# A table of 470 moved jobs in the recorded order of a gated recurrence fused with a multiplicative feed-forward layer

## The chip, the cores and the metric

The kernel runs on one core of a Trainium2 chip. The metric is device time in microseconds. Before the change the median of five runs is 530.94 us (530.24 to 532.46).

## The reference

The first stage is a gated linear recurrence over 4 sequences of 5824 steps with 256 channels; the second is a feed-forward layer without an activation, on the 23296 resulting rows.

```
a_t = exp(8 * sigmoid(r_gate) * log(sigmoid(a_param)))        # decay, per step and channel
x_gated = sqrt(max(1 - a_t*a_t, 1e-6)) * sigmoid(i_gate) * x
h = a_t * h + x_gated                                          # over the steps; y = all h
out = (((y @ w1) * (y @ w2)) @ w3) @ w_out                     # 256 -> 1024 -> 1024 -> 256
```

## The kernel before

The rows are cut into 46 chunks: chunk 0 has 256 rows, all others 512. Channels lie on the 128 partitions in two halves for the scan. The product of w3 and w_out is formed once on the chip (the "fold"), so that each chunk needs two up products of 256 by 1024 and one down product of 1024 by 256.

Every piece of work is a job, 2032 in all. For chunk c the jobs are:

- loads r, i, x on the SP queue (L171), each 512 KB; SP also issues the stores and the DMA transpositions (turn_dma, L228);
- on ACT: tanh_r and tanh_i (L179, L189), decay in two halves (the exponential, L235), root (L251, the square root, which needs another function table than tanh and exponential), four copies of an up product from PSUM (copy, L313, through L311) and two copies of the down product (evac);
- on POOL: plus and two halves of times (sigmoid of i times x, L195 to L214), two squares of the decay (L244), and the cast of y to bf16 (L288); for some early chunks DVE does times, squares or the cast;
- on DVE: gated (L261), two scans (L273), and four products g = pa * pb (L319, called product c,mp);
- on PE: turn_r and turn_u as matrix transpositions for some early chunks (L216; the others go by DMA), four pairs pa and pb of up products (L294), four downs (L326).

The fold has, for each of 8 pieces of w3, a load, a cast on POOL, fold_t (transposition on PE), fold_c (copy to SBUF on DVE), fold_m (product with w_out on PE) and fold_e (copy of the result to wp_sb on DVE, L416).

A planner inside the kernel gives each job a due time and a duration, and picks jobs for each engine by due time when their inputs and buffers are free in its own clock (L594 to L634). The list of jobs by planned start, `plan`, is then recorded job by job; nothing at run time changes the order. Each engine does its own jobs strictly in the recorded order, with waits on semaphores for inputs from other engines and for buffers. So a job that is put ahead of another on an engine holds it up if it must itself wait. SP's queue works in the same manner: a store that waits for its data holds all loads behind it.

The buffers that connect the engines: pa and pb share three PSUM buffers (tag pab), given out in recorded order; a buffer of pa is free after copy, one of pb after product. Two PSUM buffers (tag po) serve the downs, the transpositions on PE and the fold. There are 3 buffers for each of r, i, x, 6 for decay, root and the transposed u, 4 for y, 3 for g and 3 for output tiles.

A group of chunks shares one table switch: all roots of a group (for example chunks 12 to 16) stand together on ACT, and the first of them needs the squares of the whole group. Before up products in the first 80 us, small matmuls on the identity (L299) are put in where the planner saw PE idle; their number is fixed by the planner, before the table is used.

The place where the order can be altered by hand already exists; with an empty table it does nothing:

```
    places = {p for p, _ in MOVES}
    rest = [key for p, key in enumerate(plan) if p not in places]
    for p, to in MOVES:
        rest.insert(to, plan[p])
```

Of the kernel before, what the change touches and what calls it, by code (L numbers as in the profile page):

```python
# [20 lines left out]
def kernel(  # L21
# [80 lines left out]
    SLOT = 10.5  # L102
    M_OCC, M_LAT, M_PE = 0.04033835273, 0.02581866041, 0.0
    WARM = 80.0
    MOVES = []
    OFFSET = {"r": 6.5, "i": 4.0, "x": 7.5, "tanh_r": 1.5, "tanh_i": 5.0, "plus": -14.0, "turn_r": -0.5,
              "turn_u": 4.0, "decay": 10.5, "square": -2.5, "root": 8.5, "gated": 10.0, "cast": 6.5,
              "copy": 2.5, "product": -3.0, "store": 5.0}
# [531 lines left out]
    plan = [key for _, _, key in sorted(order)]  # L640
# [4 lines that stand above are left out]
# [37 lines left out]
```

## Time and profile before

| | |
|---|---|
| median of 5 runs | 530.94 us |
| profiled execution | 530.74 us, span 528.9 us |
| PE busy | 497.1 us (94%) |
| ACT busy | 456.7 us (86%) |
| DVE busy | 442.8 us (84%) |
| POOL busy | 342.4 us (65%) |
| HBM over the span | 78.91 MB read, 23.86 MB written |
| granted TensorE clock | 1.00 |

The time of the profiled execution is that of the whole run; its span goes from the first to the last instruction. In the page's slices each digit is the busy share of one fortieth of the span, about 13.2 us. A line of a timeline gives start, duration, engine, line, operation, what it writes from what it reads, and in brackets how long the engine was idle before it and what ended that. Names in the trace: ptr is a transposition on PE, ptw and pw are the fold's PSUM tiles, pa and pb the up products, po the down product, nrm the squares, roots and gated inputs, h_t the scan's result, y_t its bf16 cast, g_t the product.

### The profile page before, as it was taken

To read this page: it belongs to the slowest core of one execution; us is meant where nothing else is said; L and a number is where in the kernel's file an instruction comes from. 1 tells how busy PE (TensorE), PEld (TensorE's weight loads), DVE (VectorE), ACT (ScalarE), POOL (GpSimd) and SP (SyncE) were. 2 spreads that over 40 slices of the span, in tenths; PEclk is the share of its full clock that TensorE was granted. 3 is DMA by queue.
4 is the path that set the end of the run, shared out by engine and by line. 5 is a ranking of instruction groups with operands and counts; after the bars stand their busy time and mean duration, and the time that the engine had idled before them with its cause. 6 is when DMAs were issued, how large, how long until landed. Compare 5 with 4: busy or idle time off the path is not lost.

```text
span 528.9 us, 8756 instructions
## 1 busy us (share of the span) xinstructions
PE 497.1 (94%) x3148; PEld 308.2 (58%) x3204; DVE 442.8 (84%) x376; ACT 456.7 (86%) x535; POOL 342.4 (65%) x270
## 2 busy tenths in 40 slices
PE   1299899999999999999999999999999999999997
PEld 1176676566556566556566566565665665655555
DVE  0788899998999889997889799898798988698842
ACT  5988797999899989989989989998999998965453
POOL 1569795578747768964895968878588667492100
PEclk9999999999999999999999999999999999999999
DMA  8999969899998996998897999978999876623112
GB/s 291 387 374 360 307 161 304 244 277 251 310 259 195 311 298 190 257 240 208 238 236 236 233 319 262 259 221 218 244 261 273 239 176 163 160 77 86 57 40 100
DMA packets 174604, 123.28 MB, mean 233 GB/s; under 512 B 84448, under 2 KB 170208, under 8 KB 174560
## 3 DMA queue, kind: packets, MB, share of 16 engines
q1 hardware_dynamic: 174288, 122.71, 84.8%
q8 instruction: 25, 0.41, 0.3%
q14 instruction: 19, 0.16, 0.1%
q10 hardware_dynamic: 272, 0.00, 0.0%
HBM read 78.91 MB, written 23.86 MB: 194 GB/s over the span
## 4 chain that ended last, share of the span: by engine, by line
PE 79%; ACT 8%; DMA 4%; DVE 4%; issue 4%; SPq 0%; DVEq 0%; ACTq 0%
PE po L334 26%; PE pb L303 25%; PE pa L303 25%; DMA out_dram<-ot 2%; ACT sa L311 2%; DVE g_t L323 2%; ACT a_t L242 2%; ACT nrm L258 1%; DMA rt<-th_r 1%; PE pw L399 1%; DMA r_t<-in_r_gate_dram 1%; PE ptr L221 1%; DVE h_t L284 1%; ACT th_r L183 1%; ACT th_i L192 1%
## 5 line engine op out<-in xcount | busy, mean ns | idle before, releaser
L323 DVE TENSOR_TENSOR g_t<-sa,pb 128x1024 bf16<-128x1024 bf16 (+1 forms) x184 | 219.3, 1200 | 56.2 <-ACT sa L311 41.2
L303 PEld LDWEIGHTS <-w_sb 128*128 128x128 bf16 x1472 | 144.3, 98 | 142.8 <-issue 4.0
L311 ACT CAST sa<-pa 128x1024 bf16<-128x1024 f32 (+1 forms) x183 | 182.1, 1002 | 34.7 <-PE pa L303 32.8
L303 PE MATMUL pa<-y_t,w_sb 128*128 128x512 bf16 (+1 forms) x698 | 184.3, 378 | 3.4 <-DVE g_t L323 1.7
L303 PE MATMUL pb<-y_t,w_sb 128*128 128x512 bf16 (+1 forms) x718 | 185.8, 378 | 1.4 <-DVE g_t L323 0.3
L334 PE MATMUL po<-wp_sb,g_t 128*128 128x256 bf16 x1456 | 181.0, 273 | 0.2
L334 PEld LDWEIGHTS <-g_t 128*128 128x128 bf16 x1456 | 142.4, 98 | 45.0
L284 DVE TENSOR_TENSOR_SCAN h_t<-a_t,h_t,nrm 128x512 f32<-128x512 f32 (+3 forms) x90 | 137.1, 1535 | 0.8
L213 POOL TENSOR_TENSOR u_t<-th_i,x_t 128x512 bf16<-128x512 f32 x78 | 117.8, 1528 | 0.9 <-DMA ut<-u_t 0.5
L249 POOL TENSOR_TENSOR nrm<-a_t 128x512 f32<-128x512 f32 (+1 forms) x84 | 100.1, 1206 | 14.1 <-ACT a_t L242 12.8
L292 POOL CAST y_t<-h_t 128x1024 bf16<-128x1024 f32 x40 | 50.1, 1252 | 89.0 <-DVE h_t L284 86.2
L197 POOL TENSOR_SCALAR th_i<-th_i 128x1024 f32<-128x1024 f32 x42 | 52.3, 1248 | 35.0 <-ACT th_i L192 34.9
L311 ACT COPY ot<-po 128x512 f32<-128x512 f32 (+1 forms) x89 | 51.7, 583 | 17.1 <-PE po L334 16.9
L242 ACT ACTIVATE a_t<-rt,la 128x512 f32<-128x512 bf16 x74 | 59.0, 819 | 6.7 <-DMA rt<-th_r 6.6
L269 DVE SCALAR_TENSOR_TENSOR nrm<-nrm,ut 128x1024 f32<-128x1024 f32 x39 | 55.4, 1420 | 1.7 <-DMA ut<-u_t 1.7
L192 ACT ACTIVATE th_i<-i_t 128x1024 f32<-128x1024 f32 (+1 forms) x46 | 48.4, 1052 | 1.2 <-POOL u_t L213 1.1
L258 ACT ACTIVATE nrm<-nrm 128x1024 f32<-128x1024 f32 (+1 forms) x46 | 47.4, 1055 | 0.2
L185 ACT ACTIVATE th_r<-r_t 128x1024 bf16<-128x1024 f32 x37 | 39.2, 1063 | 0.4 <-DMA r_t<-in_r_gate_dram 0.4
L221 PE MATMUL ptr<-ident,th_r 128*128 128x128 bf16 x68 | 6.9, 259 | 15.0 <-ACT th_r L183 15.0
L258 ACT ACT_TABLE_LOAD x14 | 18.0, 1283 | 0.2
L242 ACT ACTIVATE a_t<-ptr,la 128x512 f32<-128x512 bf16 (+1 forms) x18 | 12.7, 753 | 3.6 <-PE ptr L221 3.1
L221 PEld LDWEIGHTS <-th_r 128*128 128x128 bf16 x68 | 5.4, 118 | 16.4 <-ACT th_r L183 15.8
(39 smaller groups left out, 143.5 us busy)
## 6 DMA issues: line engine op xcount, KB each, us to landing
r_t<-in_r_gate_dram SPq DMA_DIRECT2D x45, 512.0 KB, 6.1
i_t<-in_i_gate_dram SPq DMA_DIRECT2D x45, 512.0 KB, 5.5
x_t<-in_x_dram SPq DMA_DIRECT2D x45, 512.0 KB, 4.9
out_dram<-ot SPq DMA_DIRECT2D x89, 256.0 KB, 3.5
wf<-in_moe_w_dram SPq DMA_DIRECT2D x12, 512.0 KB, 6.2
wf<-in_moe_w_out_dram SPq DMA_DIRECT2D x2, 512.0 KB, 7.1
ut<-u_t SPq DMA_TRANSPOSE x39, 4.9
rt<-th_r SPq DMA_TRANSPOSE x37, 5.1
```

What stands on the lines that cost most here:

```text
L192: nc.scalar.activation(out=t[:, :n, :], in_=T["i", c][:, :n, :], func=AF.Tanh, scale=0.5)
L197: nc.gpsimd.tensor_scalar(t, t, 1.0, 1.0, op0=ALU.add, op1=ALU.mult)
L213: nc.gpsimd.tensor_mul(out=u.rearrange("p cb j q -> p j cb q")[:, js], in0=cut(t)[:, js], in1=cut(T["x", c])[:, js])
L242: nc.scalar.activation(out=a, in_=pr, func=AF.Exp, scale=la4[:, cb:cb + 1], bias=la4[:, cb:cb + 1])
L249: eng.tensor_mul(out=T["n", c][:, cb, :w], in0=T["a", c][:, cb, :w], in1=T["a", c][:, cb, :w])
L258: nc.scalar.activation(out=T["n", c][:, :, :w], in_=T["n", c][:, :, :w], func=AF.Sqrt, scale=-1.0, bias=1.0)
L269: nc.vector.scalar_tensor_tensor(out=T["n", c][:, :, :w], in0=T["n", c][:, :, :w], scalar=1e-3, in1=T["pu", c][:, :, :w], op0=ALU.max, op1 ...
L284: nc.vector.tensor_tensor_scan(T["h", c][:, cb, lo:hi], T["a", c][:, cb, lo:hi], T["n", c][:, cb, lo:hi], init, ALU.mult, ALU.add)
L303: nc.tensor.matmul(out=pp[:, q, :w], lhsT=w_sb[:, cb, m * P:(m + 1) * P], rhs=T["y", c][:, cb, :w], start=(cb == 0), stop=(cb == NCB - 1))
L311: nc.scalar.copy(out=dst, in_=src_ps)
L323: nc.vector.tensor_mul(out=T["g", c][:, 2 * mp:2 * mp + 2, :w], in0=T["sa", c, mp][:, :, :w], in1=T["pb", c, mp][:, :, :w])
L334: nc.tensor.matmul(out=po, lhsT=T["g", c][:, k, j * P:(j + 1) * P], rhs=wp_sb[:, k, :], start=(k == 0), stop=(k == KD - 1), skip_group_che ...
```

## The change

The table gets 470 entries (place in the plan, place in the new list). Each named job is taken out of the plan and put in again at the given place; all others keep their relative order. The places go up to about 703 of 2032, which is the work on the early chunks. Engine, operation and data of every job stay the same. The table's start and end:

```diff
-    MOVES = []
+    MOVES = [(2, 0), (13, 4), (16, 5), (10, 6), (18, 7), (1, 9), (7, 10), (8, 15), (23, 19), (32, 20),
+             (19, 25), (22, 26), (28, 27), (25, 28), (37, 29), (21, 31), (27, 32), (39, 33), (36, 34),
+             (24, 35), (35, 39), (33, 40), (44, 41), (45, 42), (48, 49), (56, 50), (43, 52), (61, 54),
...
+             (692, 690), (682, 694), (671, 695), (690, 696), (685, 697), (676, 700), (686, 702),
+             (669, 703)]
```

What it does to single jobs, read from the order of the two programs' instructions (a place is counted within the job's own engine; the time is that of the job in the profile before):

| engine | job | place before | place after | time before, us |
|---|---|---|---|---|
| SP | load x of chunk 0 | 1 | 9 | 0.74 |
| SP | load r of chunk 2 | 8 | 4 | 4.82 |
| SP | load x of chunk 5 | 23 | 40 | 22.75 |
| DVE | squares of chunk 2 | 5, 6 | 4, 5 | 18.74 |
| DVE | times of chunk 2 | 4 | 6 | 17.50 |
| DVE | cast of chunk 0 | 13 | 10 | 26.47 |
| DVE | square 3,0 | 15 | 19 | 28.18 |
| DVE | fold_e 5 | 47 | 45 | 59.91 |
| DVE | product 8,1 | 97 | 100 | 127.33 |
| DVE | product 10,1 | 114 | 113 | 152.09 |
| PE | pa 3,3 | 64 | 54 | 73.37 |
| PE | pa 10,0 | 144 | 139 | 142.44 |
| ACT | tanh_i of chunk 4 | 19 | 29 | 26.15 |
| ACT | root of chunk 3 | 29 | 34 | 37.04 |
| POOL | squares of chunk 12 | 61, 62 | 69, 78 | 115.72, 116.82 |

## The prediction

> **What bounds the kernel now.** I read the busy shares and slices of the page first.
>
> ```profile
> PE 497.1 (94%) x3148; PEld 308.2 (58%) x3204; DVE 442.8 (84%) x376; ACT 456.7 (86%) x535; POOL 342.4 (65%) x270
> ...
> PE   1299899999999999999999999999999999999997
> ...
> DVE  0788899998999889997889799898798988698842
> ...
> PEclk9999999999999999999999999999999999999999
> DMA  8999969899998996998897999978999876623112
> ```
>
> PE is the bound and idles almost only in the first two slices and the last. So I asked for the stretches that the moved jobs cover (they end near 185 us) and the rest.
>
> ```profile
> core 0: us, PE busy (x) PEld busy (x) DVE busy (x) ACT busy (x) POOL busy (x), PEclk, DMA share, GB/s
> 0.00:27.00 27.00, 5.99 (x47) 4.71 (x48) 11.69 (x18) 21.06 (x25) 9.84 (x15) 1.00 0.93 340
> 27.00:62.00 35.00, 32.24 (x262) 22.34 (x264) 30.45 (x38) 28.50 (x34) 26.19 (x25) 1.00 1.08 344
> 62.00:127.00 65.00, 64.18 (x434) 40.98 (x440) 58.66 (x50) 59.88 (x71) 48.23 (x36) 1.00 0.91 249
> 127.00:163.00 36.00, 34.69 (x215) 21.19 (x218) 35.61 (x29) 33.12 (x40) 21.21 (x17) 1.00 1.07 284
> 163.00:185.00 22.00, 21.89 (x132) 12.82 (x132) 20.50 (x17) 20.55 (x26) 18.00 (x15) 1.00 1.01 257
> ```
>
> PE's idle time is 21.0 us before 27, 2.8 from 27 to 62, 0.8 to 127, 1.3 to 163, 0.1 to 185: 26.0 us is all that moving early jobs can reach. From 127 to 163 DVE rests only 0.4 us, so there DVE sets the pace with PE. The lines of PE's and DVE's timelines with an idle time behind them name the rest.
>
> ```profile
> 26.30 1.03 PE L221 MATMUL ptr<-ident,th_r 128*128 128x128 bf16 x8 [3.41 <-ACT th_r L183]
> 27.12 1.27 PE L299 MATMUL pa<-ident 128*128 128x128 bf16 x10
> 28.19 1.06 PE L303 MATMUL pa<-y_t,w_sb 128*128 128x256 bf16 x4
> ...
> 60.37 0.61 PE L385 MATMUL ptw<-ident,w_t 128*128 128x128 bf16 x8 [1.43 <-DVE wp_sb L416]
> ...
> 153.35 0.81 PE L303 MATMUL pa<-y_t,w_sb 128*128 128x512 bf16 x3 [1.10 <-DVE g_t L323]
> ```
>
> ```profile
> 22.92 1.26 DVE L266 SCALAR_TENSOR_TENSOR nrm<-nrm,ptr 128x512 f32<-128x512 f32 x2
> 24.10 2.45 DVE L284 TENSOR_TENSOR_SCAN h_t<-a_t,h_t,nrm 128x512 f32<-128x512 f32 x2
> 26.47 0.40 DVE L292 CAST y_t<-h_t 128x512 bf16<-128x512 f32 x1
> 26.78 1.28 DVE L266 SCALAR_TENSOR_TENSOR nrm<-nrm,ptr 128x512 f32<-128x512 f32 x2
> 28.18 1.14 DVE L249 TENSOR_TENSOR nrm<-a_t 128x512 f32<-128x512 f32 x1
> 30.21 0.69 DVE L323 TENSOR_TENSOR g_t<-sa,pb 128x512 bf16<-128x512 bf16 x1 [0.89 <-PE pb L303]
> ```
>
> The second fence is the opening: chunk 0's scans are done at 23.0, but its cast (26.47), which the first up product needs, stands behind chunk 1's gating and scans. PE starts real work at 28.19.
>
> **The change part by part.** No instruction is added or removed, and ACT still loads 31 tables. The lowered programs differ in order alone: 153 of PE's 582 jobs, 102 of DVE's 362, 135 of ACT's 503, 62 of POOL's 264 and 114 of SP's 321 stand at another place. So the cost is in waits, and I follow the new order with the old durations.
>
> *Opening loads (SP).* x of chunk 0 goes from first to ninth, r of chunk 2 and the first two weight loads go ahead. r of chunk 0 no longer follows 0.25 MB. From the landings (ACT's first tanh 5.68 after 0.5 MB issued, second 7.01 after 1.0 MB) that is 1.33 us per 0.5 MB, so r lands 0.66 us earlier; ACT, which runs without a pause from 10.85 to 17.5, moves up by about 0.6. x of chunk 0 lands after 3.75 MB instead of first: 5.68 + 3.25 x 2.66 = 14.3; its product, which ran at 10.65, is then at 14.3. It is not late: gating needs it at 21. DVE does two squares ahead of chunk 2's product, which costs most of the 0.6 back, so gating of chunk 0 stays at about 20.95 (was 21.07). I take 0.1.
>
> *The cast of chunk 0 (DVE, three places up).* Gating 0.75, two scans 1.27, cast 0.40: it ends near 23.3 instead of 26.87, and up product 0 can start near 23.9 instead of 28.19, 4.3 earlier. This isn't yet the gain. The three PSUM buffers fill, and the second pb waits for the first gating product on DVE. DVE is late by the cast: gating and scans of chunk 1 from 23.3 to 26.85, gating of chunk 2 to 28.1, product at 28.1 instead of 30.21. Of these 2.1 us, 0.68 comes from one square put behind it. On equal work DVE is 1.4 ahead, plus up to 1.2 of its own waits for PE (0.89, 0.16 and 0.16) that go: 2.6. Following PE through pa and pb of chunk 0, its last pb starts near 32.1 (was 34.75). I take 2.1, between 1.4 and 2.6: by the DVE row, since DVE's chain releases PE's buffers.
>
> *Weight fold, 44 to 66 us.* fold_e 5 now stands ahead of products 2,2 and 2,3 (2 x 1.13 us). In the old order PE waited for it, 1.43 + 0.34 by the timeline. With the move the buffer is free 2.3 us earlier, so the wait goes, unless the weight loads are late: w3 loads are issued on SP when the previous cast frees a buffer, and one is now behind the transposed r of chunk 6, which waits for its tanh (near 44 us, old load 46.7), so not later. Between 0 and 1.8 I take 1.4, near the row.
>
> *62 to 127.* Chunk 3's products go ahead of chunk 4's scans, downs are spread, stores and loads change places on SP. PE has only 0.8 idle; the part at 103 (0.29 and 0.27) falls partly: +0.2. Late loads would cost here: x of chunk 5 goes 17 SP places back, behind a DMA transposition of chunk 4, to about 53 us with its use at 66; x of chunk 9 and r of chunks 12 to 14 keep 10 us or more. Cost nothing, while those 10 us last; if they go, POOL's product is late and the transposition after it on SP, then gating and scan.
>
> *127 to 163.* Product 10,1 now comes before the cast of chunk 11 (1.6 us), which clears the 1.10 wait at 153.35, if DVE isn't late: +0.5. Against this, product 8,1 goes behind chunk 10's two scans and a square (with them 4.1 us of DVE work), while PE wants the buffer for pa 8,3 0.7 us earlier. Old times: 127.33 - 0.97 (idle) + 4.1 + 1.2 = 131.7 for its end, against 132.04 - 0.7 = 131.3 for PE. At equal leads PE waits 0.4; laid on the old slots, 1.85. I take -1.1, the middle, as PE will lead DVE a little. On POOL the two squares of chunk 12 go 8 and 16 places back, to about 146, with the group's five roots at 149 waiting for them: no cost, 3 us of cover; past these ACT waits and the two PSUM copies behind the roots with it.
>
> *The lock.* By the tile view the scans of this stretch took
>
> ```profile
> L284 DVE TENSOR_TENSOR_SCAN h_t<-a_t,h_t,nrm x29: 1140/1283/2380, 25.3 to 187.8; 128x512 f32<-128x512 f32 x27, 128x448 f32<-128x448 f32 x2
> ```
>
> so at times 1.1 us over the median. The Trainium skill, "SBUF — State Buffer", section "SBUF: two separate sides", says that DVE operations with two SBUF inputs and GpSimd operations take a shared port pair as an exclusive lock, and the loser waits for a whole instruction. So who meets whom is drawn anew by a new order, and the old durations, which I used, need not hold. By the row the sum is unchanged; by the rule, two more stretched scans in DVE's full stretch at 127 to 163 cost 2 x 1.1 = 2.2. I take the row, since stretches can also go, and keep 2.2 both ways in the range.
>
> *Sum.* 0.1 + 2.1 + 1.4 + 0.2 + 0.5 - 1.1 = 3.2 us. After 185 us the order is the same and PE idles only 2.5 us in 315, so a lead of all engines is carried to the end. The profiled execution took 530.74 (span 528.9 and 1.8 around it), 0.2 under the median of the runs: 530.74 - 3.2 = 527.5, or 527.7 beside the median.
>
> **Rivals.** (B) The head start is lost: DVE, 30.45 of 35 us busy from 27 to 62, keeps the old pace, and PE fills the time with the same waits elsewhere. For it: 35.6 of 36 us at 127. Against it: DVE idles 10 us in all between 27 and 127, which an earlier PE removes. It gives 530.3. (C) All of it comes and nothing is given back: 2.6 + 1.8 + 0.6 + 1.1 = 6.1, 524.8. Against it: product 8,1. (D) Slower: DVE comes to 122 us without a lead of its own (late products, stretched scans), and then the order there turns against PE: waits at pa 8,3 (1.85), pb 8,3 (0.64), pa 10,0 (0.54: its cast has 3.1 us more ahead, and it is itself 4.0 us earlier on PE), pb 10,0 (0.89), pb 10,1 (0.66), as the new order on old slots has them: 4.6 us, doubled where DVE is stretched by 2.2 again, with the opening's gain down to 1.4 and the fold's to 1.4: +1.8 to +4, about 533.5. It decides where DVE's lead at product 8,0 is under 2 us.
>
> **How the numbers follow.** Forecast 0.47, its own range 526.0 to 529.2; B 0.18; C 0.10; D 0.25. The predicted time is 527.7. The range from 524.9 to 534.0 leaves half of C (0.05) and the upper third of D (0.1) outside. A measurement here tells about 0.3%, 1.6 us: faster is the forecast and C and a little of B, 0.59; same is most of B and the edge of D, 0.17; slower 0.24.
>
> **What would show it.** First up matmul with y near 24, chunk 0's first gating product near 28.1, no wait of a fold transposition for wp_sb near 60, PE's idle time from 0 to 62 down from 23.8 to about 20. A wait of pa for g_t near 130 is the give-back; many of them, with DVE full, D. Wrong would be: waits of PE for y_t casts, of ACT for rt transpositions (one of 2.77 us is in the old trace) or of SP that push loads to their use.

## The result, and the profile after

| | before | changed |
|---|---|---|
| median | 531.54 us (46 runs, 528.82 to 534.34) | 528.85 us (25 runs, 525.4 to 531.26) |
| profiled execution | 530.74 us, span 528.9 us | 527.21 us, span 525.4 us |
| PE, ACT, DVE, POOL busy, us | 497.1, 456.7, 442.8, 342.4 | 495.6, 455.7, 436.4, 342.9 |

The ratio is 0.9952, with an interval of 0.9938 to 0.9966: the changed kernel is faster by 2.6 us (1.8 to 3.3). Its profiled execution lies 1.6 us under its own median, the one before 0.8 under its own, so the two profiles differ by 3.5 us and the medians by 2.7. The readings below account for the 3.5; why typical executions keep only about 2.7 of it comes in the section on the experiments.

The longer table moves all line numbers by 65: an up product is L368, the copy of pa L376, the product g L388, a scan L349, the cast of y L357, gated L331 and L334, a square L314, tanh_r L250, decay L307, a load L239.

First the page of the changed kernel: busy times, then the slices of PE, the granted clock and the DMA share.

```profile
PE 495.6 (94%) x3147; PEld 307.2 (58%) x3204; DVE 436.4 (83%) x376; ACT 455.7 (87%) x535; POOL 342.9 (65%) x270
...
PE   1489999999999999999999999999999999999997
...
PEclk9999999999999999999999999999999999999999
DMA  8989989999999997988995999959999875633113
```

PE's first slices read 1, 4, 8 and no longer 1, 2, 9: real work begins earlier, with a hole behind it. DVE is 6.4 us less busy with the same instructions. Next the stretches of the prediction, in the changed kernel.

```profile
core 0: us, PE busy (x) PEld busy (x) DVE busy (x) ACT busy (x) POOL busy (x), PEclk, DMA share, GB/s
0.00:27.00 27.00, 8.60 (x71) 7.28 (x72) 12.33 (x17) 21.42 (x26) 9.42 (x15) 1.00 0.94 349
27.00:62.00 35.00, 31.48 (x266) 20.96 (x269) 33.66 (x40) 30.31 (x36) 29.67 (x25) 1.00 0.95 302
62.00:127.00 65.00, 64.58 (x430) 41.23 (x436) 57.64 (x54) 61.46 (x74) 43.38 (x35) 1.00 1.00 270
127.00:163.00 36.00, 34.57 (x214) 21.04 (x217) 32.20 (x29) 32.24 (x37) 24.06 (x19) 1.00 1.07 289
163.00:185.00 22.00, 21.84 (x132) 13.12 (x134) 20.19 (x18) 20.41 (x26) 17.41 (x14) 1.00 1.11 280
```

From 127 to 163 DVE now rests 3.8 us instead of 0.4. That stretch was the one with both engines full, and it no longer is.

Busy time hides how much work was done in it, so I use a second measure. A PE job should take its own pace: 0.864 us for an up product of 512 columns (four matmuls), 0.875 for a down or a product of the fold, 0.445 for a transposition of eight matmuls, half for chunk 0. The small matmuls on the identity count with 0.056 us each. The start of a job to the start of the next, less that pace, is PE time lost, whether PE idled, was held up or ran slower than its pace. Summed by stretch, in us (a loss across a boundary can be split otherwise, which moves single entries by up to 0.3):

| | 0-27 | 27-45 | 45-62 | 62-127 | 127-163 | 163-185 | 185-end | sum |
|---|---|---|---|---|---|---|---|---|
| before | 24.3 | 3.5 | 2.4 | 0.6 | 1.2 | 0.0 | 1.1 | 33.1 |
| changed | 22.4 | 4.2 | 0.5 | -0.2 | 1.8 | -0.1 | 1.1 | 29.6 |
| difference | -2.0 | +0.7 | -1.9 | -0.8 | +0.5 | -0.1 | 0.0 | -3.5 |

The sum is the whole difference of the two spans, within rounding. The places show in PE's timeline of the changed kernel, in its lines with an idle time behind them.

```profile
24.41 1.01 PE L368 MATMUL pa<-y_t,w_sb 128*128 128x256 bf16 x4 [0.27 <-DVE y_t L357]
...
29.89 0.61 PE L286 MATMUL ptr<-ident,th_r 128*128 128x128 bf16 x8 [2.30 <-DVE nrm L331]
...
42.06 1.02 PE L368 MATMUL pb<-y_t,w_sb 128*128 128x512 bf16 x4 [0.39 <-DVE g_t L388]
43.57 1.04 PE L368 MATMUL pa<-y_t,w_sb 128*128 128x512 bf16 x4 [0.48 <-DVE y_t L357]
...
145.02 1.02 PE L368 MATMUL pb<-y_t,w_sb 128*128 128x512 bf16 x4 [0.26 <-DVE g_t L388]
148.90 1.02 PE L368 MATMUL pb<-y_t,w_sb 128*128 128x512 bf16 x4 [0.25 <-DVE g_t L388]
150.63 1.02 PE L368 MATMUL pa<-y_t,w_sb 128*128 128x512 bf16 x4 [0.71 <-DVE g_t L388]
```

The first up product stands at 24.41 instead of 28.19. Then PE waits 2.30 us with a transposition of chunk 4 for a PSUM buffer, which DVE's gating frees. No fold transposition waits near 60. Two small waits at 42 and 44 are new, and so are three at 145 to 151, in place of one of 1.10 at 153. DVE's timeline of the opening in the changed kernel:

```profile
21.91 1.99 DVE L349 TENSOR_TENSOR_SCAN h_t<-a_t,nrm 128x256 f32<-128x256 f32 x2
23.93 0.43 DVE L357 CAST y_t<-h_t 128x512 bf16<-128x512 f32 x1
24.28 1.28 DVE L331 SCALAR_TENSOR_TENSOR nrm<-nrm,ptr 128x512 f32<-128x512 f32 x2
25.47 3.19 DVE L349 TENSOR_TENSOR_SCAN h_t<-a_t,h_t,nrm 128x512 f32<-128x512 f32 x2
28.58 1.25 DVE L331 SCALAR_TENSOR_TENSOR nrm<-nrm,ptr 128x512 f32<-128x512 f32 x2
29.76 0.67 DVE L388 TENSOR_TENSOR g_t<-sa,pb 128x512 bf16<-128x512 bf16 x1
```

The cast stands right behind the scans of chunk 0. But those scans took 1.99 us where the old trace has 1.27, and those of chunk 1 3.19 where it has 2.45, so the first product moved only from 30.21 to 29.76. The old line of chunk 0's scans:

```profile
21.74 1.27 DVE L284 TENSOR_TENSOR_SCAN h_t<-a_t,nrm 128x256 f32<-128x256 f32 x2
```

One thing the row of the granted clock doesn't show: it reads 1.00 from the start in both pages, but its first record lies at 31.84 us before the change and at 26.13 in the changed kernel, and PE ran at half pace until then. Four matmuls on 256 columns took 1.06 us at 28.19 before and 1.01 at 24.41 in the changed kernel. After these times they take 0.60, first in the old trace and then in the new:

```profile
33.05 0.60 PE L303 MATMUL pb<-y_t,w_sb 128*128 128x256 bf16 x4
```

```profile
30.48 0.60 PE L368 MATMUL pb<-y_t,w_sb 128*128 128x256 bf16 x4
```

Of chunk 0's eight up products four ran at half pace before, and two in the changed kernel.

The lead over the kernel before, start against start, is 3.78 us at the first up product of chunk 0 (4.25 at the ten small matmuls ahead of it), 3.57 at the first up products of chunks 14, 16 and 20, 3.58 at chunk 30, 3.53 at chunk 45, and 3.52 at the last store. Behind chunk 14 nothing is gained or lost in this profile.

### The profile page after: what moved, and what is told of

Same layout as the page of the kernel before. It is cut to its first block, busy times and chain, and to the rows that moved or that the text cites. A ratio compares the mean times of both kernels' runs of the same rounds, so it can differ in the third digit from the quotient of the medians.

```text
span 525.4 us, 8727 instructions
## 1 busy us (share of the span) xinstructions
PE 495.6 (94%) x3147; PEld 307.2 (58%) x3204; DVE 436.4 (83%) x376; ACT 455.7 (87%) x535; POOL 342.9 (65%) x270
## 4 chain that ended last, share of the span: by engine, by line
PE 81%; DVE 7%; ACT 4%; issue 3%; DMA 3%; SPq 0%; ACTq 0%; DVEq 0%
PE po L399 27%; PE pa L368 26%; PE pb L368 26%; DVE h_t L349 3%; DVE g_t L388 2%; DMA rt<-th_r 2%; ACT a_t L307 1%; ACT sa L376 1%; PE pw L464 1%; DMA r_t<-in_r_gate_dram 1%; PE ptr L286 1%; ACT th_i L257 1%; PE ptw L450 1%; DVE nrm L331 1%; DVE y_t L357 0%
## 5 line engine op out<-in xcount | busy, mean ns | idle before, releaser
L388 DVE TENSOR_TENSOR g_t<-sa,pb 128x1024 bf16<-128x1024 bf16 (+1 forms) x184 | 219.6, 1200 | 62.3 <-ACT sa L376 42.1
L368 PEld LDWEIGHTS <-w_sb 128*128 128x128 bf16 x1472 | 143.6, 98 | 142.2 <-issue 4.7
L376 ACT CAST sa<-pa 128x1024 bf16<-128x1024 f32 (+1 forms) x183 | 181.8, 1003 | 39.1 <-PE pa L368 37.9
L368 PE MATMUL pa<-y_t,w_sb 128*128 128x512 bf16 (+1 forms) x703 | 183.4, 377 | 3.6 <-DVE g_t L388 1.3
L368 PE MATMUL pb<-y_t,w_sb 128*128 128x512 bf16 (+1 forms) x712 | 184.7, 377 | 2.1 <-DVE g_t L388 0.9
L349 DVE TENSOR_TENSOR_SCAN h_t<-a_t,h_t,nrm 128x512 f32<-128x512 f32 (+3 forms) x90 | 133.2, 1494 | 0.7
L278 POOL TENSOR_TENSOR u_t<-th_i,x_t 128x512 bf16<-128x512 f32 x78 | 114.0, 1479 | 3.1 <-DMA x_t<-in_x_dram 1.6
L314 POOL TENSOR_TENSOR nrm<-a_t 128x512 f32<-128x512 f32 (+1 forms) x84 | 101.2, 1220 | 11.6 <-ACT a_t L307 10.3
L357 POOL CAST y_t<-h_t 128x1024 bf16<-128x1024 f32 x40 | 50.7, 1267 | 80.0 <-DVE h_t L349 74.4
L262 POOL TENSOR_SCALAR th_i<-th_i 128x1024 f32<-128x1024 f32 x42 | 54.9, 1309 | 41.0 <-ACT th_i L257 41.0
L376 ACT COPY ot<-po 128x512 f32<-128x512 f32 (+1 forms) x89 | 51.7, 583 | 16.9 <-PE po L399 16.8
L307 ACT ACTIVATE a_t<-rt,la 128x512 f32<-128x512 bf16 x74 | 58.6, 819 | 2.1 <-DMA rt<-th_r 2.0
L334 DVE SCALAR_TENSOR_TENSOR nrm<-nrm,ut 128x1024 f32<-128x1024 f32 x39 | 53.0, 1361 | 0.7 <-DMA ut<-u_t 0.7
L250 ACT ACTIVATE th_r<-r_t 128x1024 bf16<-128x1024 f32 x37 | 39.1, 1061 | 0.4 <-DMA r_t<-in_r_gate_dram 0.3
L307 ACT ACTIVATE a_t<-ptr,la 128x512 f32<-128x512 bf16 (+1 forms) x18 | 12.8, 753 | 3.3 <-PE ptr L286 1.9
```

Source lines behind the costliest of these rows:

```text
L262: nc.gpsimd.tensor_scalar(t, t, 1.0, 1.0, op0=ALU.add, op1=ALU.mult)
L278: nc.gpsimd.tensor_mul(out=u.rearrange("p cb j q -> p j cb q")[:, js], in0=cut(t)[:, js], in1=cut(T["x", c])[:, js])
L307: nc.scalar.activation(out=a, in_=pr, func=AF.Exp, scale=la4[:, cb:cb + 1], bias=la4[:, cb:cb + 1])
L314: eng.tensor_mul(out=T["n", c][:, cb, :w], in0=T["a", c][:, cb, :w], in1=T["a", c][:, cb, :w])
L334: nc.vector.scalar_tensor_tensor(out=T["n", c][:, :, :w], in0=T["n", c][:, :, :w], scalar=1e-3, in1=T["pu", c][:, :, :w], op0=ALU.max, op1 ...
L349: nc.vector.tensor_tensor_scan(T["h", c][:, cb, lo:hi], T["a", c][:, cb, lo:hi], T["n", c][:, cb, lo:hi], init, ALU.mult, ALU.add)
```

## The experiments

The expectations weigh three readings. By the first, the one that was predicted, each stage has its own saving, from waits that can be named, and a lead once won is carried on. By the second the order works only as a whole: a part of it meets the old order at a seam and waits there. By the third (the lock of the prediction) the order matters little, and the gain is that DVE and POOL happen to meet less at their shared ports. All edits change only the table, so that the order of the jobs alone is different. The diffs show the table's size, or the order of an engine's jobs against that of the changed kernel; "lead" is again start against start with the kernel before, in the profiles.

**The first part of the new order, then the old.** Three runs keep the new order for its first 87, 230 or 460 jobs; all jobs behind these stand in the old order.

```diff
-    MOVES = [ ... ]   # 470 entries
+    MOVES = [ ... ]   # 52 entries: the first 87 jobs as in the changed list, the rest as in plan
```

> The new order for the first 87 jobs of its list alone (to the first up product of chunk 1, about 31 us), the old order for all the rest. Theory A (each stage's saving is kept by PE): the opening saves 2.2 us by chunk 1, and 1 to 2.2 of it reach the end, since the old waits at 60 and 153 us stay: 0.2 to 0.4% faster. Theory S (a stage is worth something only with the stages that follow): under 0.5 us, same. Theory L (the gain is that DVE and POOL meet less in the shared port from 62 to 185 us): 0, with DVE's stretched operations as in the kernel before.

```diff
-    MOVES = [ ... ]   # 470 entries
+    MOVES = [ ... ]   # 150 entries: the first 230 jobs as in the changed list, the rest as in plan
```

> The new order for the first 230 jobs (to about 62 us, opening and weight fold), then the old order. A: 3.2 us saved in the profile by chunk 3's first up product (opening 2.2, less 0.8 given back at chunk 2's cast, fold 1.85), 2.5 to 3.2 in the end. S: about half of the whole change, 1.3. L: at most 0.5.

```diff
-    MOVES = [ ... ]   # 470 entries
+    MOVES = [ ... ]   # 313 entries: the first 460 jobs as in the changed list, the rest as in plan
```

> The new order for the first 460 jobs (to about 117 us), then the old order. A: 4.0 us by 127 us, then the old order's wait of pa 10,3 for product 10,1 behind chunk 11's cast, which grows with PE's lead: 2.7 to 3.5 in the end. S: nearly all, 2.5. L: most of it, because 4.1 of the 6.6 us of DVE stretch that vanished lay from 62 to 127.

| | median, us | ratio to before | lead at chunk 14, us |
|---|---|---|---|
| first 87 | 532.23 | 1.0021 (1.0007 to 1.0034) | -2.8 |
| first 230 | 533.24 | 1.0048 (1.0029 to 1.0067) | -3.3 |
| first 460 | 533.15 | 1.0035 (1.0023 to 1.0048) | -2.0 |

All three are slower than the kernel before, though each has the early first up product. With the first 87 jobs, PE waits for a copy of the fold behind two squares of chunk 3, which stand together there and took 1.57 and 1.52 us instead of the usual 0.68, while POOL ran squares as well (32.56 to 35.04). PE's line and then DVE's, of this run:

```profile
36.25 1.01 PE L390 MATMUL ptw<-ident,w_t 128*128 128x128 bf16 x8 [3.01 <-DVE w3t L399]
```

```profile
32.58 3.01 DVE L254 TENSOR_TENSOR nrm<-a_t 128x512 f32<-128x512 f32 x2
35.52 0.68 DVE L399 COPY w3t<-ptw 128x1024 bf16<-128x1024 bf16 x1
```

With the first 230, a transposition that lands at 75.81 instead of 70.89 holds ACT for 4.15 us, and PE behind the copy for 2.66. ACT's line of this run, then PE's:

```profile
75.84 0.81 ACT L259 ACTIVATE a_t<-rt,la 128x512 f32<-128x512 bf16 x1 [4.15 <-DMA rt<-th_r]
```

```profile
78.08 1.66 PE L320 MATMUL pb<-y_t,w_sb 128*128 128x512 bf16 x4 [2.66 <-ACT sa L328]
```

With the first 460, ACT's tanh_i waits 5.26 us for a buffer that POOL's times has to free (124.65), and PE waits 4.34 us at 126.66 for a copy behind it. So every seam costs more than what lies ahead of it had brought. This is the second reading, and stronger than it was put: no cut that was tried gives a share of the gain.

The seams cost more than their wait, too. The windows around the first one, in the run with 87 jobs:

```profile
33.00:36.00 3.00, 0.24 (x3) 0.07 (x1) 3.00 (x3) 2.89 (x4) 3.00 (x3) 1.00 1.03 385
36.00:39.00 3.00, 2.75 (x15) 1.84 (x15) 2.49 (x4) 0.68 (x1) 0.49 (x1) 0.52 1.07 357
39.00:42.00 3.00, 3.00 (x23) 1.63 (x22) 2.97 (x4) 1.98 (x3) 1.15 (x2) 0.91 1.07 372
```

Behind the wait the granted clock is 0.52, then 0.91: 0.48 x 3 + 0.09 x 3 = 1.7 us of PE's full pace are lost on top. The same sum is 1.7 behind the seams of the other two.

**The whole order once more.** The table is the same list of jobs, written in other lines.

> The changed kernel's order again, a second profile. If its savings come from the order, PE's lead over the kernel before is again 3.6 us at 185 us within 0.7, with the same waits. If they come from chance encounters in the shared port, the stretch of DVE's operations from 27 to 185 us (8.8 us in the first profile, 15.4 before) and the lead differ by more than 1.5 us from the first profile.

528.23 us, ratio 0.9941 (0.9922 to 0.9961): the gain stands. The profiled execution (528.32) has the same waits as the one of the changed kernel up to chunk 14, where its lead is 3.51. DVE's instructions from 27 to 185 took 9.1 us more than their usual durations (scan 1.28, gated 1.21, times 1.24, cast 0.69, square 0.68 us) against 8.8 in the changed kernel and 15.4 before, so the lower figure belongs to the order and not to one execution. But 1.4 us of lead go at chunk 15, on the part of the list that is not changed. ACT's line, then PE's:

```profile
192.74 1.06 ACT L242 ACTIVATE th_r<-r_t 128x1024 bf16<-128x1024 f32 x1 [1.77 <-DMA r_t<-in_r_gate_dram]
```

```profile
194.75 1.02 PE L360 MATMUL pb<-y_t,w_sb 128*128 128x512 bf16 x4 [0.55 <-ACT sa L368]
```

tanh_r of chunk 24 waits for its load, and the next copy and PE wait behind it. In the changed kernel's profile the same instruction waited 0.32 us:

```profile
191.22 1.06 ACT L250 ACTIVATE th_r<-r_t 128x1024 bf16<-128x1024 f32 x1 [0.32 <-DMA r_t<-in_r_gate_dram]
```

**The cast of chunk 0, alone and put back.**

```diff
-    MOVES = [ ... ]   # 470 entries
+    MOVES = [(67, 57)]
```

> The old order with one job moved: the cast of chunk 0 on DVE ahead of chunk 1's gating and scans. Theory A (DVE's chain releases PE's buffers): the first up product starts near 24.3 (3.5 us earlier; a transposition on PE ahead of it that waits for ACT may hold it at 27.1), but the first gating product stays near 30.2; 0 to 0.8 us faster. Rival (PE's start counts): 2.5 us or more faster.

530.94 us, ratio 0.9997 (0.9984 to 1.001): nothing. The cast is at 23.54, yet PE cannot use it:

```profile
26.80 1.03 PE L221 MATMUL ptr<-ident,th_r 128*128 128x128 bf16 x8 [3.41 <-ACT th_r L183]
```

In the old order the transposition of chunk 3 stands on PE ahead of the first up product and waits for its tanh as before. The cast is half of a pair; the changed order also moves that transposition.

```diff
 scan 0,1
-cast 0
 gated 1
 scan 1,0
 scan 1,1
+cast 0
 gated 2
```

> The new order with the cast of chunk 0 put back behind chunk 1's second scan. A: the first up product starts near 28.5 instead of 24.4; of these 4.1 us part was spent waiting for the first gating product, which is 0.4 earlier now: 1 to 2 us slower than the changed kernel. Rival (PE's start counts): 4 us slower.

531.36 us, ratio 0.9999 (0.9984 to 1.0014): putting this one job back takes the whole gain, 2.5 us by the median of the changed kernel and 3.1 by that of its second run. PE's line in this run:

```profile
29.28 1.01 PE L360 MATMUL pa<-y_t,w_sb 128*128 128x256 bf16 x4 [4.40 <-DVE y_t L349]
```

PE was still at half pace during this wait and until 32.25 us, 6.1 later than in the changed kernel. In this profile the lead at chunk 14 is 0.78 us instead of 3.57 or 3.51, so 2.7 to 2.8 are gone by then; another 1.8 goes at chunk 15, at the load of r of chunk 24 (the table further down). The cast is necessary for the gain and not enough for it.

**The fold's step.**

```diff
 scan 3,1
-fold_e 5
 cast 3
 product 2,2
+product 2,3
+fold_e 5
 fold_c 6
-product 2,3
 fold_c 7
```

> The new order with the fifth fold result's copy (fold_e 5) put back behind products 2,2 and 2,3 on DVE. A: the transposition of fold piece 6 on PE waits again 1.4 to 1.8 us near 58 us and that reaches the end. Rival (the wait is hidden by PE's lead or by DVE being the bound): under 0.4 us.

529.36 us, ratio 0.9962 (0.9948 to 0.9976). A wait of PE is back at the same transposition, but by another path:

```profile
61.26 0.61 PE L442 MATMUL ptw<-ident,w_t 128*128 128x128 bf16 x8 [1.54 <-ACT a_t L299]
```

In this run fold_e 5 starts at 62.07, when the transposition has begun. So PE did not wait for the buffer that fold_e 5 frees. It took the other of the two, which the decay of chunk 8 on ACT freed at 61.21. What the early fold_e 5 gives is a buffer that is free sooner than that one. The lost PE time from 45 to 62 is 2.45 us against 0.5 and 0.8 in the two profiles of the changed order: 1.7 to 2.0 in its stretch. By the medians, 0.5 to 1.1 us are left of this at the end.

**Product 8,1.**

```diff
 product 7,3
+product 8,1
 scan 10,0
+product 8,2
 scan 10,1
-product 8,1
-product 8,2
 product 9,0
```

> The new order with products 8,1 and 8,2 put back ahead of chunk 10's scans on DVE. The prediction put a give-back of 1.1 us on this place: then this kernel is 1.1 faster than the changed one. By the changed kernel's trace PE doesn't wait there: 0, or a loss where chunk 10's cast comes later.

529.73 us, ratio 0.9968 (0.9954 to 0.9982): not faster than the changed kernel. The lost PE time from 127 to 163 is 2.4 us against 1.8 and 1.3 in the two profiles of the changed order, with waits at new places (0.57 at 133.53, 0.71 at 147.40). So the new place of product 8,1 is no give-back that shows; in these profiles the old place loses 0.6 to 1.1 in its stretch.

**SP's queue alone in the old order**, all other engines in the new one (482 entries).

> The new order on the four engines, the old order in SP's queue alone (114 jobs). If the load order matters (r of chunk 0 first, weights and transpositions ahead): the opening loses 0.5, and transpositions or stores that are late for the new ACT order cost 1 us or more on top, 1 to 4 slower than the changed kernel. Rival (loads are early enough either way): under 0.7 slower.

553.18 us, ratio 1.0424 (1.0396 to 1.0452): 22 us slower than before. The waits of ACT by what it waited for (us in total, times, longest), in this run:

```profile
ACT a_t L301 <- DMA rt<-th_r: 21.8, 8, 5.2
...
ACT th_r L244 <- DMA r_t<-in_r_gate_dram: 7.2, 2, 5.1
```

and in the changed kernel:

```profile
ACT a_t L307 <- DMA rt<-th_r: 2.0, 3, 1.0
```

The order of the other engines can't run without SP's 114 moved jobs. In the old SP order transpositions stand behind stores that wait for data which now comes later: SP's longest wait ahead of a store is 8.7 us here and 6.5 in the changed kernel. What SP's moves gain by themselves this run doesn't tell.

**The squares of chunk 12 on POOL.**

```diff
 cast 8
+square 12,0
+square 12,1
 times 11,0
...
 times 13,1
-square 12,0
 plus 14
...
 square 15,1
-square 12,1
 times 15,0
```

> The new order with the two squares of chunk 12 put back 8 and 16 places on POOL, ahead of the products for u. The move's cover was put at 3 us: then this is the same within 0.5. If the move is what keeps DVE and POOL apart at 114 to 130 us, DVE's stretch from 62 to 163 us rises from 5.1 us by 1 or more and the time with it.

537.88 us, ratio 1.0135 (1.0101 to 1.0168), 9.0 to 9.7 us above the changed kernel. POOL's timeline and then PE's, in this run:

```profile
118.99 1.04 POOL L306 TENSOR_TENSOR nrm<-a_t 128x512 f32<-128x512 f32 x1 [6.31 <-ACT a_t L299]
120.90 1.71 POOL L306 TENSOR_TENSOR nrm<-a_t 128x512 f32<-128x512 f32 x1 [0.87 <-ACT a_t L299]
122.57 7.68 POOL L270 TENSOR_TENSOR u_t<-th_i,x_t 128x512 bf16<-128x512 f32 x4
130.20 1.04 POOL L349 CAST y_t<-h_t 128x1024 bf16<-128x1024 f32 x1
```

```profile
131.29 1.87 PE L360 MATMUL pa<-y_t,w_sb 128*128 128x512 bf16 x4 [6.15 <-POOL y_t L349]
```

The decays of chunk 12 are 3.4 and 3.8 us later in the changed order (117.79 and 119.71 instead of 114.43 and 115.93), while POOL is there earlier. At the old place the squares wait for them, and the cast of chunk 9, which PE needs, stands behind. The late place is thus what the rest of the order needs.

**x of chunk 0 loaded first, as before.**

```diff
+load x 0
 load r 0
...
 load i 1
-load x 0
 load x 1
```

> The new order with one load put back: x of chunk 0 first in SP's queue. A: r of chunk 0 lands 0.66 us later, ACT's opening chain moves by it: 0.4 to 0.7 slower in the profile at the first up product, and 0 to 0.6 in the end.

530.49 us, ratio 0.9982 (0.9963 to 1.0002): 1.6 to 2.3 us above the changed kernel. In the profile the lead at chunk 0's first up product is 2.80 us instead of 3.78, and 3.23 in the second profile of the changed order: by single profiles 0.4 to 1.0 us of it come from the opening loads. PE left its half pace at 29.00 us in this run.

**A scan one step further up**, meant to take the three waits at 145 to 151 away.

```diff
 gated 11
+scan 11,0
 product 9,2
 product 9,3
-scan 11,0
 product 10,0
```

> A version meant to be better: the changed order with chunk 11's first scan put two places up on DVE, into the 1.22 us in which DVE waits for PE ahead of product 9,2. PE's waits at 144 to 151 us (1.7 us lost in the changed kernel's trace) fall by 1.2: 1.2 faster than the changed kernel. Rival: something else is then last (copies on ACT, the table switch ahead of the roots at 142): under 0.3.

529.06 us, ratio 0.9955 (0.9933 to 0.9977): no gain over the changed kernel. Of the three waits one of 0.21 stays, and one of 1.15 at 139.88 is new. The lead at chunk 14 is 5.29 us in this profile, the largest of all, since its opening also happened to run better (lost time from 27 to 45: 2.1 against 4.2). It didn't last: at chunk 16 the lead is 1.38. ACT's line, then PE's, then the windows, all of this run:

```profile
192.09 1.06 ACT L242 ACTIVATE th_r<-r_t 128x1024 bf16<-128x1024 f32 x1 [2.90 <-DMA r_t<-in_r_gate_dram]
```

```profile
194.09 1.02 PE L360 MATMUL pb<-y_t,w_sb 128*128 128x512 bf16 x4 [1.69 <-ACT sa L368]
195.35 1.84 PE L360 MATMUL pa<-y_t,w_sb 128*128 128x512 bf16 x4 [0.23 <-DVE g_t L380]
```

```profile
192.00:195.00 3.00, 1.31 (x6) 0.48 (x5) 0.93 (x1) 2.90 (x3) 0.00 (x0) 1.00 1.16 331
195.00:198.00 3.00, 2.77 (x10) 1.31 (x9) 3.00 (x4) 2.99 (x5) 1.37 (x1) 0.57 1.10 349
198.00:201.00 3.00, 3.00 (x22) 2.13 (x20) 1.90 (x2) 2.92 (x4) 3.00 (x4) 0.86 1.22 271
```

It is the load of r of chunk 24 again. The table compares its issue on SP with the start of the tanh:

| profile | r of chunk 24 issued | tanh_r of chunk 24 starts | ACT waited | lead at chunk 14, then 16 |
|---|---|---|---|---|
| before | 189.61 | 194.84 | 0.36 | - |
| changed | 186.22 | 191.22 | 0.32 | 3.57, 3.57 |
| again | 187.53 | 192.74 | 1.77 | 3.51, 2.12 |
| x of chunk 0 first | 188.25 | 193.51 | 1.65 | 2.61, 1.35 |
| product 8,1 put back | 189.54 | 194.60 | 1.80 | 1.68, 0.26 |
| fold_e 5 put back | 190.63 | 195.71 | 2.24 | 1.01, -0.85 |
| cast of chunk 0 put back | 190.93 | 195.92 | 2.22 | 0.78, -1.05 |
| scan 11,0 up | 186.51 | 192.09 | 2.90 | 5.29, 1.38 |

The tanh starts 5.0 to 5.6 us behind the issue in all eight, with a DMA share of 1.1 to 1.2 there. Before the change the load was already just in time, so a lead passes this point only as far as SP's queue is ahead as well. Of these seven profiles with the new order, whole or but for one change, the changed kernel's own is the only one that loses nothing here. In the changed kernel's profile SP was 3.4 ahead, in the last one 3.1 while PE was 5.3 ahead. Why SP follows less than PE in most executions is open.

**Profile and median.** This also bears on the 1.6 us between the changed kernel's profile and its median: an execution that loses 1.4 us at chunk 15, as the second profile does, is at 528.3. A second part is the clock. Each run also has its mean granted clock: 8 of the changed kernel's 25 runs had 0.996 or 0.997, with a median of 530.15, the other 17 had 0.999 or 1.0, with 528.21 (of 53 runs of the kernel before, 9 were at 0.996 or 0.997). One loss of 1.7 us in 525 is 0.003. Two profiles with the new opening, those of the fold's step and of product 8,1, show where: behind PE's wait near 29.9 (2.25 and 1.93 us in them). The windows of the fold's step put back:

```profile
27.00:30.00 3.00, 0.75 (x8) 0.54 (x7) 3.00 (x4) 2.03 (x4) 1.86 (x3) 0.94 1.01 340
30.00:33.00 3.00, 3.00 (x19) 2.35 (x18) 1.71 (x3) 0.37 (x1) 1.75 (x2) 0.50 0.89 301
```

The changed kernel's profile has 1.00 in the same windows, behind a wait of 2.30. That PE time is lost in part only (27 to 45: 5.2 and 4.7 against 4.2), since PE still waits for DVE there. How much of the 1.6 each part makes was not measured.

## Why the prediction was right

The forecast was 527.5 for the profiled execution and 527.7 for the median; they came at 527.21 and 528.85. The sign and the size hold, and the main mechanism too: the early cast, by way of DVE, and the fold's buffer. That the profile is met to 0.3 is in part luck. The opening gave less than forecast, the two next stretches gave more, the fourth lost as much as forecast by another cause, and this profile happened to keep its whole lead at chunk 15. Point by point:

- *Opening loads and the cast (0.1 + 2.1).* The opening gave 2.0 up to 27 us, and the first up product was 3.8 earlier against 4.3 forecast. But the first product is at 29.76 and not at 28.1, because four scans took 1.46 us more than in the old trace: two of them began while POOL ran, a meeting of the kind that the row on the lock put at 0. The wait that this leaves was of a transposition for a PSUM buffer of the gating, not of a second pb. Chunk 0's last pb started at 33.20 and not near 32.1. Another 0.7 was lost by 45: the changed kernel has waits of 2.30, 0.39 and 0.48 there, the last for the cast of chunk 2 (1.58 us, 2.5 us later than before). The old kernel had waits of 0.27 and 0.51 and, as an estimate, 2.4 us lost to the half pace from 27 to 31.84. The steps had no term for the later cast and none for the pace. Net, the stretch to 45 gave 1.3. PE's idle time from 0 to 62 fell from 23.8 to 21.9, not to about 20. The split was wrong as well: the loads, put at 0.1, are worth 0.4 to 1.0 of the lead, as x of chunk 0 put back alone shows; the estimate had taken most of the earlier landing away again for two squares.
- *Weight fold (1.4).* 1.9 measured, about the upper end of 1.8. A PSUM buffer that is free earlier is the mechanism forecast: with fold_e 5 put back, the same transposition waits 1.54 us at 61.26, for the other buffer.
- *62 to 127 (0.2).* 0.8 measured. DVE's instructions were stretched less there: 2.6 us over their usual durations in this stretch instead of 6.7. That this made the difference was not shown.
- *127 to 163 (+0.5 - 1.1).* The sum of -0.6 met the measured -0.5, by another cause. The step that product 8,1 makes PE wait at pa 8,3 failed: DVE was at product 8,0 at 117.08 instead of 122.14, 5.1 us ahead, and product 8,1 began at 125.85 where the working had its end at 131.7. Putting it back brings no gain. The loss is at 145 to 151: PE waits there for products of chunk 10, which stand on DVE behind the two scans of chunk 11 (2.07 and 2.85 us), and DVE's lead is down to 2.2 us at product 10,0.
- *The lock.* The row was taken, 0, with 2.2 both ways. DVE's stretch from 27 to 185 fell from 15.4 to 8.8 us, so it went, and the prediction had kept this side open. It isn't enough for a gain: the first 460 jobs have 9.2 and are slower than before, and with the cast of chunk 0 put back it is about 9 as well, at the old time. How much of the gain needs it was not shown. That the stretches come from meeting POOL is shown by the profiles, in the last section, and agrees with the exclusive lock in the section "SBUF: two separate sides" of the Trainium skill's "SBUF — State Buffer".
- *Squares of chunk 12 (no cost, 3 us of cover).* No cost, but the reason was wrong: the move isn't a free one inside a cover, it is needed, and undoing it costs 9 us.
- *"A lead of all engines is carried to the end."* This failed in general. It held to 0.05 us in one profile; in the second profile of the same order 1.4 of 3.5 us went at chunk 15, in four runs with one change 1.3 to 1.9 us, and in the run with the moved scan 3.9 of 5.3. The load of r of chunk 24 had no slack before the change, and the prediction looked for late loads only among the moved ones.

Of the rivals, C (all of it) fell by the opening, B (lost head start) by the fold and the full lead at chunk 14. D turns on DVE's lead at product 8,0, below 2 us; it was 5.1.

## What to carry to other kernels

A static order on several queues is judged as a whole: one job taken from it, or a cut at any point, tests a seam and not the share of that job, so a part that does nothing alone can carry the whole gain. Ahead of a forecast that a lead is carried to the end, look along the unchanged part for the first instruction that already starts just behind its load; the lead ends there unless the loading queue leads as well. A wait of PE of about 2 us or more has to be priced with the clock that may follow it. And where a DVE instruction takes longer than others of its shape, look at what POOL ran when it began.

## What the runs showed of the hardware

- PE's waits of 1.69 (moved scan), 1.93, 2.25, 2.66, 3.01 and 4.34 us were followed by a granted clock of about one half, for a loss of 1.7 us of full pace in each. Waits of 2.30 and 2.54 in the two profiles of the changed order weren't, nor one of 2.38 in the run with 230 jobs. One of 6.15, with the squares of chunk 12 put back, was followed by 6.8 us of half clock. The Trainium skill's "TensorE: Matmul & The Clock Gate", section "Part 1: The HAM clock gate (the "warmup" mystery)", tells of a free-running window of 3.4 us and a half clock after an idle one. The size agrees, half of 3.4 being 1.7, and the chance from one execution to the next fits a free-running window; but here waits of 1.7 to 2.3 us, shorter than that window, were enough at times.
- PE began at half pace in all 14 profiles (transpositions on 128 columns 0.107 us apart, later 0.056) and left it between 24.8 and 32.3 us, in the profile before at 31.84 and in the two of the changed order at 26.13 and 25.66. The profile's clock reads 1.00 there, so the pace has to be read from the matmuls.
- A scan's time isn't set by its size alone, but by what POOL runs when it begins. Two scans of 64 columns in the changed kernel, in DVE's timeline, and POOL's line beside them:

```profile
143.60 0.26 DVE L349 TENSOR_TENSOR_SCAN h_t<-a_t,nrm 128x64 f32<-128x64 f32 x1
...
146.43 1.30 DVE L349 TENSOR_TENSOR_SCAN h_t<-a_t,nrm 128x64 f32<-128x64 f32 x1
```

```profile
144.29 4.52 POOL L278 TENSOR_TENSOR u_t<-th_i,x_t 128x512 bf16<-128x512 f32 x3 [1.57 <-DMA x_t<-in_x_dram]
```

The first scan ran while POOL was idle. The second began while POOL was in one of these products, which ended 1.15 us later, and the scan ended 0.15 us after it. The long scans keep to this as well: of the changed kernel's 84 scans of 512 columns, 32 took 1.34 us or more, and each of these ended 1.07 to 1.08 us behind the POOL instruction that ran at its start. None of the other 52 began with more than 0.24 us of a POOL instruction still to go. From 27 to 185 us all 18 DVE instructions that took over 0.1 us more than usual began while POOL ran; before the change it was 26 of 27, and in the last POOL began 0.02 us later. So DVE waited there for POOL's instruction to end, and the changed order has fewer such meetings.
